# Bias rows of an attention kernel: twelve relu tiles moved to GpSimd, copies, relus and the first round dealt out anew

## The chip, the cores and the metric

The kernel runs on one core of a Trainium2 chip. The metric is device time in microseconds (us) for one launch; the median of three runs before the change is 658.66 us (657.89 to 660.17). PE is TensorE's matmul, PEld its weight load, DVE is VectorE, ACT is ScalarE, POOL is GpSimd, and SP issues most DMAs.

## The reference

The computation is attention with an additive bias that a small network makes from positions, followed by a feed-forward layer.

```python
scores = scale * np.matmul(q, k.transpose(0, 1, 3, 2))      # 4 batches, 8 heads, 576 x 576, head size 64
rel = (pos[:, None] - pos[None, :])
psi_rel = np.log1p(np.abs(rel))
psi_i = np.log1p(np.maximum(pos[:, None], 1.0))
x = (psi_rel / psi_i)[..., None]
h = np.maximum(x @ w1 + b1, 0.0)                            # 32 hidden units per pair of positions
bias = h @ w2                                               # 8 heads
scores = scores + bias.transpose(2, 0, 1)[None]
attn = softmax(scores);  out = attn @ v
# then, over 2304 tokens: h = x @ w_in (512 -> 2048), softplus(h), @ w_out (2048 -> 512)
```

## The kernel before

**Bias stage.** The bias is the same for all batches, so it is made once, for 576 query rows, in 36 sets of 16 rows. Dividing by `psi_i` is pulled out of the relu: for each group of four rows (a *quarter*, `g` 0 to 3, of set `s`) one relu tile `m` = max(lw + pb1, 0) is computed over the distances (`lw` has w1 times log1p of the distance, 128 partitions are 4 rows by 32 hidden units). That is 144 tiles of 304 to 576 columns. VectorE computes them (line 216), except those listed in `RELU_ACT`, which ScalarE computes (line 214). TensorE multiplies the four tiles of a set by the weights (line 243) into a PSUM tile `acc`, of which there are two. Then `emit_rows` copies `acc` to an SBUF tile `e`, times 1/psi_i: on ScalarE (line 267), or on VectorE (line 265) for the pieces in `EDVE`. A set in `MIR` (*mirrored*) is written by TensorE as a row of 591 columns in both directions, and one copy of 591 columns takes it; any other set is written once, and two copies take its two directions (591 columns together). A DMA (line 275) writes `e` to DRAM (`e_d`); the attention rounds read their bias tiles `b` from there, shifted row by row.

The order on every engine is the order of the program: nothing is rescheduled later. Set `s+1` is multiplied, set `s` copied, and the relus of set `s+5` are issued (`LEAD`) in each pass of the loop. `EARLY` says after which set a bias tile is loaded, and `STAGE` at which sets nine score tiles of the first round are put in between: D computes the softmax part (VectorE adds bias and takes the maximum, line 381; ScalarE exponentiates, line 399), R only copies the raw scores out (ScalarE, line 374).

**Rounds.** Sixteen rounds follow, one for each batch and pair of heads. A round is a string of tokens, written out by hand or by a search, that fixes the order on all engines: `Zt/b` and `St/b` are the score matmuls of tile t into PSUM buffer b (this round's and the next one's), `ZAt`/`At` VectorE's bias and maximum, `ZXt`/`Xt` ScalarE's exponential, `Tjc/b` six transposes on TensorE, `Vjc/a` or `/d` their copy to SBUF (tile `pt`) on ScalarE or VectorE (lines 332, 334), `Pj` the product with the values (line 486), `L`/`ZL` a small copy on GpSimd (line 416). Round 0 (`ROUND0`) has its own string, which also finishes the tiles that the bias stage began and begins those of round 1. Its tile 4 needs the bias rows of the last four sets. From round 1 on all rounds have the same string. The feed-forward layer follows on about 370 us of TensorE work.

Of the kernel before, what the change touches and what calls it, by code (L numbers as in the profile page):

```python
# [50 lines left out]
SETS = ((2, 4), (3, 8), (7, 5, 6), (1, 0))  # L51

ROUND0 = """
q Z7/0 S1/1 T10/o ZA7 A1 v1 Z3/0 T00/2 ZX7 ZA3 k S3/1 T20/0 V10/a X1 ZL2 T30/o A3 V30/d V00/a V20/a
Z8/0 A2 S8/1 ZX3 ZL1 X3 ZA8 T40/1 V40/a w S0/2 A8 A0 ZX8 X2 Z4/0 T32/0 ZA4 T12/o ZL3 T22/2 S4/1
V22/d X0 V12/d T02/1 ZX4 I V02/d V32/a v T01/2 L0 T11/o b V01/a V11/a T21/2 A5 R/0 A4 P0 A7 A6 V21/a
C X4 P1 ZL4 T31/2 X5 L4 X8 X6 T41/1 P2 L3 G L1 V31/d X7 L2 V41/d
"""

ROUND14 = """  # L60
# [41 lines left out]
NEAR = ("wi13", "wi14", "wi15", "wi3")  # L102
LEAD = 5

RELU_ACT = {(22, 2), (4, 3), (9, 2), (17, 3), (28, 3), (30, 3), (10, 3), (2, 2), (32, 3), (1, 3), (6, 2), (21, 3), (14, 3), (5, 3), (32, 2), (7, 3), (18, 3), (29, 3), (34, 2), (22, 3), (5, 2), (0, 3), (11, 3), (25, 2), (13, 3), (16, 2), (15, 3), (18, 2), (26, 3), (31, 2)}

LOAD_AT = {}
ORD = (0, 1, 2, 3, 4, 5, 6, 7, 8, 13, 9, 10, 11, 12, 14, 15, 16, 17, 18, 19, 20, 21, 22, 23, 24, 25, 26, 27, 28, 29, 30, 31, 32, 33, 34, 35)
MIR = (0, 1, 3, 4, 5, 6, 7, 8, 10, 13, 14, 15, 16, 18, 19, 21, 22, 24, 25, 29, 30, 33, 34, 35)
EDVE = {(34, 1), (24, 1), (27, 1), (33, 0), (35, 1), (7, 0), (29, 0), (19, 0), (14, 0), (8, 0), (3, 0), (27, 0)}  # L110
EARLY = ((24, 0), (12, 5), (21, 1), (17, 6), (27, 2), (26, 7), (33, 3), (35, 8))
STAGE = """
12:R12 21:R15 23:R16 23:R17 26:D06 28:D00 30:D01 32:D05 32:D02
"""


# [1 line left out]
def tile_log_bias_attention__then__softplus_ffn(  # L118
# [13 lines left out]
    nc = tc.nc  # L132
# [68 lines left out]
        return max(16 * s + 15, S - 1 - 16 * s) + 1  # L201

    hid, accs = {}, {}

    def emit_hid(j):
        if j >= 36:
            return
        s = ORD[j]
        w = width(s)
        for g in range(4):  # L210
            i = 4 * s + g
            m = mk.tile([128, S], F32, tag="m", name="m")
            if (s, g) in RELU_ACT:
                nc.scalar.activation(m[:, :w], lw[:, :w], AF.Relu, bias=pb1[:, i:i + 1])
            else:
                nc.vector.tensor_scalar(  # L216
                    m[:, :w], lw[:, :w], pb1[:, i:i + 1], 0.0, op0=ALU.add, op1=ALU.max
                )
            hid[s, g] = m

    def emit_mm(j):
# [33 lines left out]
    def emit_rows(j):  # L255
# [80 lines left out]
    def u_s(n, t):  # L336
# [41 lines left out]
        def first():  # L378
            m = st.tile([128, 1], F32, tag="m", name="m", bufs=12)
            st_["m"] = m  # L380
            nc.vector.tensor_tensor_reduce(  # L381
                prob[n, t].rearrange("p (a c) -> p a c", a=2),
                st_["ps"],
                bias[pr, t].rearrange("p (a c) -> p a c", a=2),
                op0=ALU.add,
                op1=ALU.min,
                scale=-0.125,
                scalar=3.0e38,
                accum_out=m,
            )  # L390
# [179 lines left out]
    def flush():  # L570
        run([((), None)] * 40)
# [497 lines left out]
```

## Time and profile before

| what | value |
|---|---|
| median of three runs | 658.66 us |
| profiled execution | 658.76 us, span 656.9 us |
| bias stage (first relu to last copy) | 5.4 to 55.6 us |
| round 0 up to its first product with the values | 55.6 to 66.9 us |
| PE busy over the span | 639.8 us, 97% |
| DVE, ACT, POOL busy over the span | 499.2, 509.1, 33.0 us |

Times in the trace count from the start of the span. A busy share over the whole span says little here: TensorE is full from 67 us on, and the change concerns what stands before. In a row that gives windows, each engine's busy time stands with the number of its instructions; in a row of waits stand the total, the times and the longest; a group of instructions shows busy time and the mean of one in ns, then the idle time before them.

### The profile page before, as it was taken

The page shows a single profiled execution, that of the slowest core. Times are in us where ns is not written, and L with a number is a line of the kernel's source. Part 1 is how long each engine was busy: PE and PEld are TensorE (multiplying, and loading weights), DVE is VectorE, ACT ScalarE, POOL GpSimd, SP SyncE. Part 2 cuts the span into 40 slices and gives each one's busy share as a digit, 9 for nine tenths or more (in the row PEclk, how much of TensorE's full clock was granted, in tenths as well). Part 3 has the DMA queues.
Part 4 walks back from the last instruction along what each step waited for, and adds up shares of the span by engine and source line. Part 5 has one row for each costly group of instructions (what it writes and reads, how often), then busy time and mean ns, then how long its engine had stood idle before and what let it go on. Part 6 is the DMA issues. An engine that isn't in the chain of part 4 may idle for free.

```text
span 656.9 us, 13575 instructions
## 1 busy us (share of the span) xinstructions
PE 639.8 (97%) x4992; PEld 483.2 (74%) x4992; DVE 499.2 (76%) x1081; ACT 509.1 (77%) x1034; POOL 33.0 (5%) x104
## 2 busy tenths in 40 slices
PE   6898999999999999999999999999999999999997
PEld 3334666766766766888888888888888888888886
DVE  7998799999999997896976847785964656556554
ACT  6998899999999997986877758866775665755653
POOL 0001111111111110000000000000000000000000
PEclk9999899999999999999999999999999999999999
DMA  6797889888886645752223004210201403202220
GB/s 223 274 312 251 287 257 315 266 257 277 274 257 231 192 155 177 234 204 95 100 96 121 8 30 165 96 65 32 81 16 56 132 7 113 80 1 88 73 97 32
DMA packets 51762, 98.97 MB, mean 151 GB/s; under 512 B 7520, under 2 KB 19440, under 8 KB 51696
## 3 DMA queue, kind: packets, MB, share of 16 engines
q1 hardware_dynamic: 51408, 98.03, 44.6%
q8 instruction: 39, 0.64, 0.4%
q14 instruction: 27, 0.22, 0.1%
q10 hardware_dynamic: 288, 0.07, 0.0%
HBM read 67.98 MB, written 28.01 MB: 146 GB/s over the span
## 4 chain that ended last, share of the span: by engine, by line
PE 95%; DMA 2%; DVE 1%; ACT 1%; issue 0%; SPq 0%; DVEq 0%; ACTq 0%
PE h L781 30%; PE y L839 30%; PE o L486 12%; PE s L363 6%; PE acc L243 5%; PE s L427 4%; PE t L363 3%; PE t L427 2%; DMA e_d<-e 1%; PE o L363 1%; PE o L427 1%; ACT e L267 1%; DMA wts<-in_mlp_dram 0%; DMA b<-e_d 0%; DVE p L381 0%
## 5 line engine op out<-in xcount | busy, mean ns | idle before, releaser
L839 PE MATMUL y<-wo,g 128*128 128x512 f32 x864 | 209.7, 390 | 0.0
L839 PEld LDWEIGHTS y<-wo,g 128*128 128x128 f32 x864 | 161.3, 188 | 33.4 <-DVE g L813 0.2
L781 PE MATMUL h<-x,wi 128*128 128x512 f32 (+1 forms) x768 | 169.6, 370 | 0.0
L781 PEld LDWEIGHTS h<-x,wi 128*128 128x128 f32 x768 | 136.2, 189 | 26.3 <-issue 0.5
L804 DVE SCALAR_TENSOR_TENSOR u<-u,e 128x512 f32<-128x512 f32 (+1 forms) x80 | 51.0, 638 | 102.5 <-ACT l L801 102.2
L399 ACT ACTIVATE p<-p,m 128x576 f32<-128x576 f32 x144 | 110.3, 767 | 4.4 <-DVE m L381 2.8
L797 ACT ACTIVATE e<-h 128x512 f32<-128x512 f32 (+1 forms) x80 | 44.3, 554 | 76.4 <-PE h L781 76.3
L486 PE MATMUL o<-pt,vn 128*64 128x256 f32 (+3 forms) x640 | 82.0, 421 | 0.0
L381 DVE CUSTOM_DVE_ANT_0 p<-s,b 128x576 f32<-128x576 f32 x83 | 61.3, 754 | 4.0 <-PE s L363 1.6
L811 ACT ACTIVATE g<-l 128x512 fp32r<-128x512 f32 (+1 forms) x80 | 46.8, 585 | 19.7 <-DVE l L808 9.8
L486 PEld LDWEIGHTS o<-pt,vn 128*64 128x64 f32 (+1 forms) x640 | 37.8, 137 | 28.0 <-issue 8.7
L363 PE MATMUL s<-kn,qn 64*128 64x288 f32 (+1 forms) x412 | 57.3, 413 | 0.7 <-ACT pt L332 0.4
L813 DVE TENSOR_TENSOR g<-l,g 128x512 fp32r<-128x512 f32 (+1 forms) x80 | 50.4, 629 | 3.7 <-ACT g L811 3.7
L808 DVE TENSOR_TENSOR l<-l,u 128x512 f32<-128x512 f32 (+1 forms) x80 | 50.6, 632 | 0.0
L806 DVE SCALAR_TENSOR_TENSOR l<-h,l 128x512 f32<-128x512 f32 (+1 forms) x80 | 50.5, 631 | 0.0
L332 ACT ACTIVATE pt<-s 128x384 f32<-128x384 f32 x93 | 44.3, 484 | 7.2 <-ACT r L537 4.9
L801 ACT ACTIVATE l<-u 128x512 f32<-128x512 f32 (+1 forms) x80 | 47.1, 589 | 2.9 <-DVE g L813 0.3
L800 ACT ACTIVATE u<-e 128x512 f32<-128x512 f32 (+1 forms) x80 | 47.2, 590 | 2.6
L798 ACT ACTIVATE e<-e 128x512 f32<-128x512 f32 (+1 forms) x80 | 47.2, 590 | 2.5
L243 PE MATMUL acc<-m,coef 128*32 128x512 f32 (+41 forms) x544 | 40.8, 429 | 8.5 <-DVE m L216 6.0
L427 PEld LDWEIGHTS s<-ident,p 64*128 64x128 f32 x654 | 31.1, 138 | 14.7 <-DVE m L381 8.4
L216 DVE TENSOR_SCALAR m<-lw,pb 128x576 f32<-128x576 f32 (+17 forms) x114 | 41.3, 440 | 0.0
(67 smaller groups left out, 750.9 us busy)
## 6 DMA issues: line engine op xcount, KB each, us to landing
e_d<-e SPq DMA_DIRECT2D x36, 295.5 KB, 3.5
qn<-in_q_dram SPq DMA_DIRECT2D x16, 576.0 KB, 6.6
b<-e_d SPq DMA_DIRECT2D x32, 288.0 KB, 3.9
r<-in_moe_w_in_dram SPq DMA_DIRECT2D x16, 512.0 KB, 5.0
r<-in_moe_w_out_dram SPq DMA_DIRECT2D x16, 512.0 KB, 3.8
xr<-x_d SPq DMA_DIRECT2D x28, 256.0 KB, 4.7
vn<-in_v_dram SPq DMA_DIRECT2D x16, 320.0 KB, 5.4
kn<-in_k_dram SPq DMA_DIRECT2D x16, 288.0 KB, 7.4
```

The lines of the kernel that those rows point to most:

```text
L243: nc.tensor.matmul(acc[32 * g:32 * g + 32, lo:hi], lhsT=coef.rearrange("p o h -> p (o h)"), rhs=m[:, d:d + hi - lo] if up > 0 else m[:, d ...
L363: nc.tensor.matmul(ps[at:at + w, half, :SH], lhsT=q_n[n][rows, hd, c0:c0 + w], rhs=k_n[n][rows, hd], start=True, stop=True, tile_position= ...
L381: nc.vector.tensor_tensor_reduce(prob[n, t].rearrange("p (a c) -> p a c", a=2), st_["ps"], bias[pr, t].rearrange("p (a c) -> p a c", a=2), ...
L399: nc.scalar.activation(p, p, AF.Exp, bias=st_["m"], scale=-1.0, accum_out=ssum[n][:, PLACE.index(t):PLACE.index(t) + 1],)
L427: nc.tensor.transpose(ps[:, a, i], src[rows], ident[rows, 64 * a:64 * a + 64], tile_position=(64 * a, 0))
L486: nc.tensor.matmul(o[up, half, 0:w], lhsT=v_n[n][rows, jb, hd], rhs=pt[n, jb][rows, c0:c0 + w], start=(jb == 0), stop=(jb == 4), tile_posi ...
L781: nc.tensor.matmul(ps[:, :nb], lhsT=wi[f][:, a, 128 * c:128 * c + 128], rhs=xs[bi, c][:, x_, :nb], start=(i == 0), stop=(i == 11),)
L804: nc.vector.scalar_tensor_tensor(u, u, -1.0, e, op0=ALU.add, op1=ALU.subtract)
L806: nc.vector.scalar_tensor_tensor(l, ps, 0.0, l, op0=ALU.max, op1=ALU.add)
L808: nc.vector.tensor_tensor(l, l, u, op=ALU.subtract)
L813: nc.vector.tensor_tensor(g[:, 1], l, g[:, 0], op=ALU.subtract)
L839: nc.tensor.matmul(y, lhsT=g[:, a, 128 * ts:128 * ts + 128], rhs=wo[f][:, w_], start=(first and i == 0), stop=(last and i == 2),)
```

## The change

Twelve relu tiles (`BESIDE`: loop pass, set, quarter) go to GpSimd. `beside()` issues those that are due, just ahead of a VectorE operation that reads PSUM (a copy in `EDVE` or a D tile's line 381) or else at the end of the pass; each is made to wait for the VectorE relu that was issued last before it (`held[-1]`). The other tables are dealt out anew: VectorE has 99 relus (114 before), ScalarE 33 (30), GpSimd 12 (0); `RELU_ACT` has a few entries that no longer apply, since `BESIDE` comes first. 26 sets are mirrored (24), so there are 46 copies (48): 37 on ScalarE (43) and 9 on VectorE (5). `EARLY`, `STAGE` and `ROUND0` are rearranged; the number of D tiles (five) and R tiles (four) in the stage is the same.

```diff
 ROUND0 = """
-q Z7/0 S1/1 T10/o ZA7 A1 v1 Z3/0 T00/2 ZX7 ZA3 k S3/1 T20/0 V10/a X1 ZL2 T30/o A3 V30/d V00/a V20/a
+Z7/0 S1/2 T10/o T00/1 ZA7 A1 A2 Z3/0 ZA3 ZX7 S3/1 Z8/0 k v1 ZL2 V10/a A3 T30/2 V30/d q X1 w V00/a
...
-RELU_ACT = {(22, 2), (4, 3), (9, 2), (17, 3), (28, 3), (30, 3), (10, 3), (2, 2), (32, 3), (1, 3), (6, 2), (21, 3), (14, 3), (5, 3), (32, 2), (7, 3), (18, 3), (29, 3), (34, 2), (22, 3), (5, 2), (0, 3), (11, 3), (25, 2), (13, 3), (16, 2), (15, 3), (18, 2), (26, 3), (31, 2)}
+RELU_ACT = {(4, 3), (28, 3), (0, 2), (8, 3), (33, 2), (13, 2), (32, 3), (1, 3), (15, 2), (26, 2), (21, 3), (4, 2), (12, 3), (17, 2), (19, 2), (10, 2), (32, 2), (1, 2), (16, 3), (29, 3), (12, 2), (20, 3), (23, 2), (14, 2), (5, 2), (27, 2), (29, 2), (9, 3), (31, 2), (33, 3), (13, 3), (24, 3), (35, 3), (7, 2), (26, 3), (20, 2)}
+BESIDE = ((17, 20, 2), (19, 21, 2), (23, 26, 2), (18, 22, 3), (20, 23, 0), (32, 35, 0), (21, 27, 0), (19, 22, 1), (24, 27, 3), (33, 35, 3), (27, 30, 0), (29, 33, 0))
+AFTER = mybir.DependencyInfo(mybir.DependencyClass.Sync, mybir.DependencyReason.ANTI)
-MIR = (0, 1, 3, 4, 5, 6, 7, 8, 10, 13, 14, 15, 16, 18, 19, 21, 22, 24, 25, 29, 30, 33, 34, 35)
+MIR = (0, 2, 3, 4, 5, 6, 7, 8, 10, 11, 12, 13, 14, 15, 16, 21, 22, 25, 26, 27, 29, 30, 32, 33, 34, 35)
-EDVE = {(34, 1), (24, 1), (27, 1), (33, 0), (35, 1), (7, 0), (29, 0), (19, 0), (14, 0), (8, 0), (3, 0), (27, 0)}
+EDVE = {(12, 1), (27, 1), (8, 0), (19, 0), (32, 0), (29, 1), (12, 0), (23, 0), (3, 0), (14, 0), (5, 0), (25, 0), (24, 1), (35, 1), (29, 0), (22, 0), (28, 1), (11, 0), (0, 0), (24, 0), (15, 0)}
-EARLY = ((24, 0), (12, 5), (21, 1), (17, 6), (27, 2), (26, 7), (33, 3), (35, 8))
+EARLY = ((23, 0), (10, 5), (18, 1), (19, 6), (29, 2), (26, 7), (33, 3), (35, 8))
-12:R12 21:R15 23:R16 23:R17 26:D06 28:D00 30:D01 32:D05 32:D02
+13:R15 20:D05 23:R12 24:R16 26:D06 27:R17 30:D01 31:D00 33:D02
...
+    def beside():
+        for s, g in queued.pop(now[0], ())[:]:
+            w = width(s)
+            i = 4 * s + g
+            m = mk.tile([128, S], F32, tag="m", name="m")
+            u = nc.gpsimd.tensor_scalar(
+                m[:, :w], lw[:, :w], pb1[:, i:i + 1], 0.0, op0=ALU.add, op1=ALU.max
+            )
+            tc.add_manual_dep(
+                u.ins, held[-1].ins.name, AFTER, reason="the port that both engines use"
+            )
+            hid[s, g] = m
...
+            if any(b[1:] == (s, g) for b in BESIDE):
+                continue
...
-                nc.vector.tensor_scalar(
+                held.append(nc.vector.tensor_scalar(
...
             if (s, part) in EDVE:
+                beside()
...
         def first():
             m = st.tile([128, 1], F32, tag="m", name="m", bufs=12)
             st_["m"] = m
+            beside()
...
+        now[0] = s
         emit_rows(s)
...
+        beside()
     flush()
```

GpSimd, from its last instruction of the set-up to the first small copies of round 0. `kn` is a one-column write that holds a load back, `m` a relu tile, `tl` a small copy of a probability tile `p`. Before:

```order
L294 COPY kn<-wts 128x1
L416 COPY tl<-p 128x128 x5
L416 COPY tl<-p_1031 128x128
L416 COPY tl<-p_1058 128x128
L416 COPY tl<-p 128x128 x3
```

Now:

```order
L316 COPY kn<-wts 128x1
L216 ISA
L216 TENSOR_SCALAR m<-lw,pb_112 128x336
L216 TENSOR_SCALAR m<-lw,pb_112 128x368
L216 TENSOR_SCALAR m<-lw,pb_112 128x352
L216 TENSOR_SCALAR m<-lw,pb_112 128x368
L216 TENSOR_SCALAR m<-lw,pb_112 128x384
L216 TENSOR_SCALAR m<-lw,pb_112 128x448
L216 TENSOR_SCALAR m<-lw,pb_112 128x432
L216 TENSOR_SCALAR m<-lw,pb_112 128x448
L216 TENSOR_SCALAR m<-lw,pb_112 128x496
L216 TENSOR_SCALAR m<-lw,pb_112 128x544
```

Two more relus of 576 columns follow, then the small copies as before; the row without a shape (ISA) stood ahead of line 673 before and now stands right behind the set-up.

VectorE in the middle of the stage, where the relus of sets 22 to 28 (368 to 464 columns) stand; `e<-acc` is a copy out of PSUM, `p,m<-s,b` a D tile. Before:

```order
L216 TENSOR_SCALAR m<-lw,pb_112 128x368 x2
L216 TENSOR_SCALAR m<-lw,pb_112 128x384 x4
L216 TENSOR_SCALAR m<-lw,pb_112 128x400 x4
L216 TENSOR_SCALAR m<-lw,pb_112 128x416 x3
L216 TENSOR_SCALAR m<-lw,pb_112 128x432 x3
L216 TENSOR_SCALAR m<-lw,pb_112 128x448 x4
L216 TENSOR_SCALAR m<-lw,pb_112 128x464 x3
L265 TENSOR_SCALAR e<-acc,tab 128x591
```

Now:

```order
L237 TENSOR_SCALAR m<-lw,pb_112 128x368 x2
L237 TENSOR_SCALAR m<-lw,pb_112 128x384 x2
L287 TENSOR_SCALAR e<-acc,tab 128x272
L237 TENSOR_SCALAR m<-lw,pb_112 128x400 x3
L237 TENSOR_SCALAR m<-lw,pb_112 128x416 x4
L237 TENSOR_SCALAR m<-lw,pb_112 128x432 x2
L404 ISA p,m<-s_83,b 128x576
L404 ISA m 128x1
L237 TENSOR_SCALAR m<-lw,pb_112 128x448
L287 TENSOR_SCALAR e<-acc,tab 128x208
L237 TENSOR_SCALAR m<-lw,pb_112 128x464 x3
```

Two copies and a D tile now stand between 17 relus, where 23 relus stood without a break.

ScalarE at the end of the stage. `e<-acc` are its last copies, `p,ss<-p,m` exponentials, `pt<-o` the first copy of transposes. Before:

```order
L267 ACTIVATE e<-acc,tab 128x591
L399 ACTIVATE p,ss_117<-p,m 128x576
L267 ACTIVATE e<-acc,tab 128x80
L267 ACTIVATE e<-acc,tab 128x511
L267 ACTIVATE e<-acc,tab 128x64
L267 ACTIVATE e<-acc,tab 128x527
L399 ACTIVATE p,ss_117<-p,m 128x576
L267 ACTIVATE e<-acc,tab 128x591
L399 ACTIVATE p,ss_117<-p,m 128x576 x4
L332 ACTIVATE pt<-o 128x2x3x64
```

Now:

```order
L289 ACTIVATE e<-acc,tab 128x591
L422 ACTIVATE p,ss_117<-p,m 128x576
L289 ACTIVATE e<-acc,tab 128x80
L289 ACTIVATE e<-acc,tab 128x511
L289 ACTIVATE e<-acc,tab 128x591 x3
L422 ACTIVATE p,ss_117<-p,m 128x576 x4
L354 ACTIVATE pt<-o 128x2x3x64
```

The copy of set 34, which VectorE made before, is now the third of the three and stands ahead of the four exponentials.

## Rows read from the trace of the kernel before

**Rows 1.** The page: the chain that ended last, shares by engine.

```profile
PE 95%; DMA 2%; DVE 1%; ACT 1%; issue 0%; SPq 0%; DVEq 0%; ACTq 0%
```

**Rows 2.** Windows: length; busy PE, PEld, DVE, ACT, POOL; clock, DMA share, GB/s.

```profile
5.40:55.60 50.20, 47.15 (x588) 19.13 (x588) 47.85 (x131) 46.15 (x87) 0.29 (x1) 1.00 0.81 287
...
46.20:55.60 9.40, 9.40 (x134) 4.02 (x132) 8.56 (x21) 8.10 (x18) 0.29 (x1) 1.00 0.80 289
55.60:66.90 11.30, 8.41 (x112) 5.18 (x110) 9.34 (x25) 9.28 (x24) 1.47 (x5) 0.98 0.79 268
```

**Rows 3.** Waits from 14 to 48 us: total, times, longest.

```profile
PEld acc L243 <- ACT e L267: 11.7, 21, 1.3
...
DVE e L265 <- PE acc L243: 1.5, 1, 1.5
ACT e L267 <- ACT e L267: 1.1, 2, 0.8
```

**Rows 4.** Groups of instructions in the stage, 5.4 to 55.6 us.

```profile
L216 DVE TENSOR_SCALAR m<-lw,pb 128x576 f32<-128x576 f32 (+17 forms) x114 | 41.3, 440 | 0.0
...
L267 ACT ACTIVATE e<-acc,tab 128x591 f32<-128x591 f32 (+22 forms) x43 | 25.5, 630 | 3.2 <-ACT e L267 1.4 <-PE acc L243 1.4 <-ACT m L214 0.2
L214 ACT ACTIVATE m<-lw,pb 128x496 f32<-128x496 f32 (+15 forms) x30 | 19.0, 661 | 3.4 <-DVE pb L192 3.4
...
L265 DVE TENSOR_SCALAR e<-acc,tab 128x591 f32<-128x591 f32 (+2 forms) x5 | 3.5, 707 | 2.0 <-PE acc L243 2.0
```

**Rows 5.** Groups by shape, 0 to 60 us: widest and narrowest copies.

```profile
L267 ACT ACTIVATE e<-acc,tab 128x591 f32<-128x591 f32 x21 | 15.7, 759 | 2.4 <-PE acc L243 1.4 <-ACT e L267 0.8 <-ACT m L214 0.2
...
L267 ACT ACTIVATE e<-acc,tab 128x47 f32<-128x47 f32 x1 | 0.3, 292 | 0.0
...
L265 DVE TENSOR_SCALAR e<-acc,tab 128x591 f32<-128x591 f32 x3 | 2.5, 832 | 2.0 <-PE acc L243 2.0
...
L265 DVE TENSOR_SCALAR e<-acc,tab 128x144 f32<-128x144 f32 x1 | 0.4, 363 | 0.0
```

**Rows 6.** Timeline of POOL: start, length; two operations of the relu's kind.

```profile
74.34 0.61 POOL L673 TENSOR_SCALAR a<-a 128x512 f32<-128x512 f32 x1 [1.90 <-ACT a L670]
...
87.03 0.61 POOL L673 TENSOR_SCALAR a<-a 128x512 f32<-128x512 f32 x1 [0.84 <-ACT a L670]
```

**Rows 7.** The chain of waits from 52 to 75 us: start, length.

```profile
55.58 3.81 DMA e_d<-e
...
59.53 2.74 DMA b<-e_d
...
63.64 0.76 DVE p L381
...
64.44 0.48 ACT p L399
...
66.92 3.54 PE o L486 x16
```

**Rows 8.** Timeline of ACT at the end of the stage.

```profile
52.44 0.78 ACT L399 ACTIVATE p<-p,m 128x576 f32<-128x576 f32 x1
...
53.19 0.77 ACT L399 ACTIVATE p<-p,m 128x576 f32<-128x576 f32 x1
...
56.26 0.78 ACT L399 ACTIVATE p<-p,m 128x576 f32<-128x576 f32 x1 [1.45 <-DVE m L381]
```

**Rows 9.** Timeline of DVE: its copy of set 34.

```profile
53.63 0.83 DVE L265 TENSOR_SCALAR e<-acc,tab 128x591 f32<-128x591 f32 x1 [0.24 <-PE acc L243]
```

**Rows 10.** Groups by shape, 0 to 130 us: copies of transposes on ACT.

```profile
L332 ACT ACTIVATE pt<-s 128x384 f32<-128x384 f32 x31 | 14.8, 485 | 2.4 <-ACT r L537 1.8 <-PE s L427 0.7
```

**Rows 11.** Timeline of PE: sixteen matmuls of one line, twice.

```profile
66.85 3.60 PE L486 MATMUL o<-pt,vn 128*64 128x256 f32 x16
...
74.29 1.89 PE L486 MATMUL o<-pt,vn 128*64 128x256 f32 x16
```

**Rows 12.** Windows around that stretch, columns as in rows 2.

```profile
66.40:69.80 3.40, 3.40 (x22) 1.93 (x24) 2.66 (x8) 2.55 (x8) 0.29 (x1) 0.50 1.00 382
```

More of the change, by code (lines that the diff above doesn't have):

```diff
@@ L53 @@
 ROUND0 = """
-q Z7/0 S1/1 T10/o ZA7 A1 v1 Z3/0 T00/2 ZX7 ZA3 k S3/1 T20/0 V10/a X1 ZL2 T30/o A3 V30/d V00/a V20/a
-Z8/0 A2 S8/1 ZX3 ZL1 X3 ZA8 T40/1 V40/a w S0/2 A8 A0 ZX8 X2 Z4/0 T32/0 ZA4 T12/o ZL3 T22/2 S4/1
-V22/d X0 V12/d T02/1 ZX4 I V02/d V32/a v T01/2 L0 T11/o b V01/a V11/a T21/2 A5 R/0 A4 P0 A7 A6 V21/a
-C X4 P1 ZL4 T31/2 X5 L4 X8 X6 T41/1 P2 L3 G L1 V31/d X7 L2 V41/d
+Z7/0 S1/2 T10/o T00/1 ZA7 A1 A2 Z3/0 ZA3 ZX7 S3/1 Z8/0 k v1 ZL2 V10/a A3 T30/2 V30/d q X1 w V00/a
+T20/0 S8/1 ZX3 ZL1 ZA8 X3 S0/o T40/2 X2 V20/a A8 ZX8 Z4/1 V40/a A0 T12/2 X0 V12/a T22/o ZA4 S4/1
+V22/d ZX4 ZL3 L0 T02/o v T32/0 V32/d T01/2 I b V02/a T11/o V01/a V11/a R/1 ZL4 C A5 A7 G T21/0 A4
+V21/a P0 A6 X8 P1 X5 X4 X6 T41/1 T31/0 L3 X7 L1 L2 P2 V41/d L4 V31/d
 """
@@ L203, in tile_log_bias_attention__then__softplus_ffn @@
     hid, accs = {}, {}
+    held, queued = [], {}
+    for at, s, g in BESIDE:
+        queued.setdefault(at, []).append((s, g))
+    now = [0]
+    def beside():
[10 more added lines that the diff above has]
+            hid[s, g] = m
     def emit_hid(j):
@@ L215, in emit_hid @@
             else:
-                nc.vector.tensor_scalar(
+                held.append(nc.vector.tensor_scalar(
                     m[:, :w], lw[:, :w], pb1[:, i:i + 1], 0.0, op0=ALU.add, op1=ALU.max
-                )
+                ))
             hid[s, g] = m
```

## The prediction

> **What bounds the kernel now.** I read the chain of waits first. TensorE has 95% of it [rows 1]; its last 590 us are full rounds and the feed-forward layer, and no line of the diff touches their order. What can move is the time at which round 0 hands TensorE its first product with the values, 66.9 us in this trace [rows 7]. Everything behind that shifts as a block. So I cut the time before it into windows [rows 2]: the bias stage (50.2 us) and round 0 up to that product (11.3 us).
>
> In the stage three engines look full: PE 47.15, DVE 47.85, ACT 46.15 of 50.2 us. PE's number deceives. The table of waits shows why: between 14 and 48 us its weight loads stand for 11.7 us, in 21 pieces, behind ScalarE's copy of line 267 [rows 3]. TensorE has two acc tiles, so set s+2 cannot begin until set s is copied, and that copy waits its turn between ScalarE's relus. VectorE and ScalarE are therefore the bound: at 47.85 / 50.2 = 95% and 46.15 / 50.2 = 92% they have 2.35 and 4.05 us to spare. In the last stretch, 46.2 to 55.6 us, TensorE never idles (9.40 of 9.40), while ACT has 1.3 us left.
>
> From the end of the stage to the product there is one chain [rows 7]: the last set's DMA to DRAM (55.58, 3.81 us), the load of bias tile 4 (59.53, 2.74 us), its maximum on VectorE (63.64), its exponential on ScalarE (64.44), transposes and copies, the product at 66.92. So a shorter stage is passed on whole, as long as the engines keep up with that chain.
>
> **The change part by part.**
>
> *VectorE.* It loses 15 relus: 41.3 us / 114 = 0.362 us each [rows 4], −5.4 us. It gains four copies; counted from the tables, its copies go from 2364 to 3898 columns. A copy costs (832 − 363) / (591 − 144) = 1.05 ns a column and 0.21 us besides [rows 5], of which some 0.09 us lies under its neighbour (an instruction's successor starts about that much before it ends). So 1534 columns and four starts are 1.6 + 0.5 = +2.1 us. Net −3.3 us.
>
> *ScalarE.* Three more relus: 661 ns less an overlap of 0.10 us, 0.56 us each [rows 4], +1.7 us. Six copies fewer with 1534 columns less: (759 − 292) / (591 − 47) = 0.86 ns a column and 0.25 us besides, 0.15 without the overlap [rows 5]: −1.3 − 0.9 = −2.2 us. Net −0.5 us.
>
> *The stage.* Together the two engines lose 3.8 of 94.0 us. At the same joint fill (94.0 of 100.4 us) the stage would be 90.2 / 94.0 of 50.2 us, which is 48.2: −2.0 us. The bounds come from the same rows. If ScalarE keeps its own fill of 92%, 45.65 / 0.919 gives 49.65 us, −0.55. If it is filled as VectorE was, 45.65 / 0.953 gives 47.9, −2.3. I take −2.0, nearer the second end, because VectorE, with 3.3 us less to do, can take the copies as they come, and because the unbroken run of 23 relus there is cut by two copies and a D tile, so that fewer sets wait for a ScalarE that is in the middle of its relus.
>
> *TensorE.* By the widths of the tables its columns in sets 27 to 35, where it never idles, go from 4907 to 5113. The last window (9.40 us) holds six sets and five score tiles, so a set of 591 takes under 1.57 us and 206 columns under 0.55 us; the other end is 0, where TensorE waits anyway. I take +0.1, since the score tiles have a large share of that window.
>
> *GpSimd.* Twelve tiles of 444 columns in the mean. Its operation of the same kind takes 0.61 us at 512 columns, both times the same [rows 6]: at most 7.3 us in a stage in which it now does nothing. By the table each is issued two to six passes before its set is multiplied, and a pass takes 50.2 / 36 = 1.4 us: being late by less than 2.8 us costs nothing. The waits stand in GpSimd's own queue, and nothing but the next relus is queued behind them until round 0's small copies. What a VectorE relu costs beside a GpSimd one no row shows: between nothing and a full stop for 7.3 us. I take 1 us, since by the tables seven of the twelve have an operation that reads PSUM next on VectorE; VectorE's 3.3 us cover it. Cost on the path: 0.
>
> The row without shape (ISA) that now stands behind the set-up stood before line 673. That operation's first run took 0.61 us like the second, and its wait of 1.90 us was for ScalarE's input [rows 6]; so I price it at nothing. The Trainium skill (GPSIMD Engine Reference, 2.1 Instruction dispatch) says that the first call after such a load pays about 6 us that no profile row shows. These rows leave no more than the 1.90 us for it; what the Trainium skill's figure would make of the time is the last rival.
>
> *Round 0.* It holds the same kinds of tokens in another order. Between its last copy of the stage and tile 4's exponential ScalarE has ten exponentials, as before, and five copies of transposes instead of four, but also set 34's copy. All of that fits into the time it idles there [rows 2], if the waits allow it. I take 0, with the third rival as the upper end and, as the lower, 0.8 us for the idle time that a better order could save.
>
> *Sum.* −2.0 + 0.1 = −1.9 us on the profiled 658.76 (span 656.9 and 1.9 around it): 656.9. The median of the three runs is 0.1 us under that execution, so **656.8 us**.
>
> **The rivals.**
>
> 1. *ScalarE stays the bound.* For it: TensorE's waits name ScalarE's copies, not VectorE's relus, and ScalarE is relieved by 0.5 us alone. Against: four copies leave its queue for VectorE at the very places where it bursts. Then −0.55 + 0.1: 658.2 us.
>
> 2. *The half-speed stretch goes.* From 66.4 to 69.8 us the granted clock is 0.50 [rows 12], the 1.2 GHz level, after a stretch in which PE was busy for 8.41 of 11.30 us. Sixteen products took 3.60 us there and 1.89 us a round later [rows 11]: 1.7 us lost, on the path. If the product starts 2 us earlier or round 0 is denser, TensorE may be busy enough not to be slowed. Against: the transposes before it are as thin as ever. Then 656.8 − 1.7 = 655.1 us.
>
> 3. *ScalarE late in round 0, slower than before.* Place: set 34's copy now stands on ScalarE ahead of four exponentials. VectorE began that copy at 53.63, when TensorE was done [rows 9], while ScalarE's exponentials began at 52.44 [rows 8]. From 53.63 on ScalarE has the copy (0.65), ten exponentials at 53.19 − 52.44 = 0.75 us [rows 8] and five copies of transposes (four at 485 − 100 ns, one narrower, 1.8 us [rows 10]): 63.6 us, only 0.8 before the 64.44 of the chain. It idled for 0.8 + 2.0 us there (from 54.81, the end of its wait of 1.45 us less that wait [rows 8], and in the round [rows 2]). If all of that idle time returns, the exponential comes at 66.4 and the product 2.0 us late; with rival 1's stage the result is 658.2 + 2.0 = 660.2. It decides as soon as the idle time kept is over 0.8 us. Against: that idle time was waiting for a chain that ScalarE was ahead of, so most of it should be swallowed.
>
> 4. *GpSimd stops VectorE.* If each of the twelve stops VectorE for its length, VectorE has −3.3 + 7.3 = +4.0 us, 1.65 more than its 2.35 us of idle time: 658.76 + 1.65 = 660.4. That five of the twelve have VectorE relus next, three of them released at one time, speaks for a part of it. The Trainium skill (SBUF — State Buffer, Who interferes with whom) gives the rule: VectorE's fast SBUF mode and GpSimd share one pair of ports, and the second to start waits for the whole of the first; an operation with one SBUF input outside that mode is free of it. By it only the unsheltered tiles count, some five times 0.5 us, and the sum on the path stays 0. No row of this trace has the two side by side.
>
> 5. *The first GpSimd tile is late.* Set 20's tile is issued in pass 17, so its start-up may cost 4.2 us (three passes) before TensorE stands still; every us beyond is one on the path. For the rows' 1.90 us that is nothing. By the 6 us of the Trainium skill (GPSIMD Engine Reference, 2.1 Instruction dispatch), as an estimate, it is 6 − 4.2 = 1.8 us, and the time 658.6 us.
>
> **How the numbers follow.** The forecast has 0.46, rival 1 0.14, rival 2 0.21, rival 3 0.11, rivals 4 and 5 0.04 each. About 0.3% (2.0 us) is what a measurement of this kernel can tell from no change, so faster means below 656.7 and slower above 660.6. The forecast sits on the first line: 0.22 of it falls under and 0.24 over. Faster: 0.22 + 0.20 of rival 2 + 0.01 = 0.43. Slower: half of rivals 3 and 4 (0.07) and 0.03 for a second half-speed stretch (+1.7 us): 0.10. The rest, 0.47, is no change. The range leaves out the far ends: from rival 2 less 0.4 to rival 3 less 0.4, **654.7 to 659.8**.
>
> **What would show it.** Right: the last copy ends near 53.6 us, the waits of weight loads for ScalarE's copies between 14 and 48 us fall well under 11.7, GpSimd's tiles take 0.45 to 0.7 us and end before TensorE wants them, the product starts near 65. Wrong: ScalarE fuller than 95% with the last copy still past 55 (rival 1); no window at clock 0.5 (rival 2); idle PE before the product with ScalarE as releaser (rival 3); VectorE relus far longer than 0.5 us beside GpSimd (rival 4). A first product that starts where it did would make the whole prediction wrong.

## The result

The kernel after the change takes 663.85 us (median of 6 runs, 662.10 to 665.38) against 658.45 us (6 runs) for the kernel before: a ratio of 1.0077, 95% interval 1.0063 to 1.0092. It is slower by 5.4 us. The forecast was 656.8 us, 654.7 to 659.8, with a chance of 0.10 for slower: wrong in sign, and the time lies outside the range.

In the profile after (span 662.0 us), first the chain that ended last, as in [rows 1]:

```profile
PE 90%; DMA 4%; ACT 2%; DVE 1%; issue 1%; POOL 1%; SPq 0%; DVEq 0%; ACTq 0%
```

TensorE's share of the chain fell from 95% to 90%, and GpSimd is on it. Next the windows of the stage, which now lasts to 60.4 us, and of the stretch with the low clock, with the columns of [rows 2] and [rows 12]:

```profile
5.40:60.40 55.00, 48.88 (x604) 19.27 (x604) 48.25 (x121) 45.92 (x84) 23.23 (x13) 1.00 0.76 264
...
66.00:70.00 4.00, 3.70 (x36) 2.01 (x36) 2.95 (x9) 4.00 (x13) 0.74 (x3) 0.62 0.80 232
```

The last copy ends at 60.35 us, not 55.55. The first product with the values, on which the prediction hung the whole time, starts 5.6 us later than in [rows 11]:

```profile
72.49 2.16 PE L509 MATMUL o<-pt,vn 128*64 128x256 f32 x16
```

The span is 5.1 us longer, so what stands behind that product did shift nearly as a block. In the stage TensorE was idle for 6.1 us (55.00 − 48.88) where it had been for 3.05. The fifth number points to the cause: POOL is busy for 23.23 us, against 0.29. The groups of GpSimd's relus (30 to 60 us) and of VectorE's (30 to 56 us) in after:

```profile
L216 POOL TENSOR_SCALAR m<-lw,pb 128x368 f32<-128x368 f32 (+8 forms) x12 | 22.9, 1924 | 30.4 <-ACT e L289 25.7 <-PE acc L264 3.1 <-DVE m L237 1.6
...
L237 DVE TENSOR_SCALAR m<-lw,pb 128x416 f32<-128x416 f32 (+13 forms) x34 | 16.7, 553 | 0.0
```

And VectorE's group of before from 30 to 56 us:

```profile
L216 DVE TENSOR_SCALAR m<-lw,pb 128x384 f32<-128x384 f32 (+13 forms) x44 | 17.0, 460 | 0.0
```

A GpSimd tile takes 1.92 us in the mean; the prediction had 0.61 at most. The last two rows say more: VectorE has ten relus fewer in that stretch and saves 0.3 us, because each became longer (553 ns against 460). The waits from 30 to 60 us (total, times, longest) name the new releaser, which [rows 3] did not have:

```profile
PEld acc L264 <- POOL m L216: 3.9, 4, 1.5
...
PE acc L264 <- POOL m L216: 2.4, 4, 1.0
```

The chain of after, where [rows 7] had one DMA of 3.81 us and one of 2.74, has longer ones; the load at 58.06 of a bias tile waits for the rows issued at 53.14:

```profile
42.73 2.37 POOL m L216
...
53.14 4.84 DMA e_d<-e
...
58.06 5.14 DMA b<-e_d
```

Up to set 20 TensorE begins the sets within about 1 us of the trace of before; from then on the relu that ends last in sets 20 to 23, 26, 27, 30, 33 and 35 is GpSimd's. Its last one ended at 58.18 us, TensorE's last product of the stage a microsecond later. The chain above leaves the stage earlier, with the rows issued at 53.14 us: it passes tiles of the eight that stand back to back and none of the last four.

### The profile page after: what moved, and what is told of

Its sections match the earlier page's. It is cut to its first block, busy times and chain, and to the rows that moved or that the text cites. A ratio compares the mean times of both kernels' runs of the same rounds, so it can differ in the third digit from the quotient of the medians.

```text
span 662.0 us, 13590 instructions
## 1 busy us (share of the span) xinstructions
PE 641.4 (97%) x5008; PEld 483.6 (73%) x5008; DVE 498.7 (75%) x1069; ACT 508.6 (77%) x1032; POOL 56.0 (8%) x116
## 4 chain that ended last, share of the span: by engine, by line
PE 90%; DMA 4%; ACT 2%; DVE 1%; issue 1%; POOL 1%; SPq 0%; DVEq 0%; ACTq 0%
PE h L804 30%; PE y L862 30%; PE o L509 11%; PE s L385 6%; PE s L450 4%; PE t L385 3%; PE acc L264 3%; PE t L450 1%; DMA b<-e_d 1%; PE o L385 1%; ACT e L289 1%; DMA e_d<-e 1%; PE o L450 1%; DMA r_d<-r 1%; POOL m L216 1%
## 5 line engine op out<-in xcount | busy, mean ns | idle before, releaser
L509 PE MATMUL o<-pt,vn 128*64 128x256 f32 (+3 forms) x640 | 80.6, 416 | 0.0
L264 PE MATMUL acc<-m,coef 128*32 128x512 f32 (+44 forms) x560 | 42.3, 420 | 11.5 <-DVE m L237 6.1
L264 PEld LDWEIGHTS acc<-m,coef 128*32 128x32 f32 x560 | 15.9, 114 | 35.8 <-issue 11.7
L385 PEld LDWEIGHTS s<-kn,qn 64*128 64x128 f32 (+1 forms) x408 | 31.4, 172 | 13.9 <-issue 4.6
```

Of the source, the lines that this page charges most:

```text
L264: nc.tensor.matmul(acc[32 * g:32 * g + 32, lo:hi], lhsT=coef.rearrange("p o h -> p (o h)"), rhs=m[:, d:d + hi - lo] if up > 0 else m[:, d ...
L385: nc.tensor.matmul(ps[at:at + w, half, :SH], lhsT=q_n[n][rows, hd, c0:c0 + w], rhs=k_n[n][rows, hd], start=True, stop=True, tile_position= ...
L509: nc.tensor.matmul(o[up, half, 0:w], lhsT=v_n[n][rows, jb, hd], rhs=pt[n, jb][rows, c0:c0 + w], start=(jb == 0), stop=(jb == 4), tile_posi ...
```

## The experiments

Theory A said that the form of GpSimd's operation is slow by itself, B that GpSimd and VectorE disturb each other, C that the new deal loses without GpSimd. The table gives each kernel's median, that of the kernel before on the same chip, and the ratio with its interval; e4, run once to time single forms, has no ratio.

| kernel | us | before | ratio |
|---|---|---|---|
| e1 twelve tiles on VectorE | 663.30 | 658.76 | 1.0060 (1.0047 to 1.0073) |
| e2 twelve tiles on GpSimd, all else old | 661.66 | 658.76 | 1.0046 (1.0031 to 1.0062) |
| e3 constant instead of the column | 663.46 | 658.76 | 1.0066 (1.0054 to 1.0078) |
| e5 new round 0 alone | 658.98 | 658.76 | 0.9997 (0.9985 to 1.0009) |
| e6 new stage alone, tiles on VectorE | 661.77 | 658.76 | 1.0038 (1.0024 to 1.0051) |
| e7 maximum with a column | 665.18 | 658.76 | 1.0087 (1.0068 to 1.0106) |
| e8 after with the old round 0 | 662.22 | 658.76 | 1.0057 (1.0038 to 1.0076) |
| e9 after with clamps | 661.65 | 658.37 | 1.0049 (1.0036 to 1.0062) |
| e10 tiles issued early | 665.74 | 658.37 | 1.0107 (1.0091 to 1.0122) |
| e11 before with clamps | 657.98 | 658.37 | 1.0004 (0.9990 to 1.0019) |
| e12 e9, old score tiles and round 0 | 659.49 | 658.96 | 1.0011 (0.9993 to 1.0028) |
| e13 e11 with new score tiles | 662.46 | 658.96 | 1.0044 (1.0027 to 1.0061) |
| e14 e9 with the old round 0 | 660.67 | 658.96 | 1.0022 (1.0013 to 1.0032) |
| e15 e9, 32 tiny matmuls first | 661.79 | 658.87 | 1.0049 (1.0036 to 1.0063) |
| e16 e6, 32 tiny matmuls first | 661.81 | 658.87 | 1.0044 (1.0031 to 1.0057) |
| e17 before, 100 tiny matmuls first | 664.10 | 658.87 | 1.0082 (1.0067 to 1.0096) |

**e1, e2: the change halved.**

```diff
+RELU_ACT -= {b[1:] for b in BESIDE}     # e1
+BESIDE = ()
```

e2 is the kernel after with `RELU_ACT`, `MIR`, `EDVE`, `EARLY`, `STAGE` and `ROUND0` of before.

> The kernel after, with its twelve GpSimd relus given to VectorE instead; copies, relus on ScalarE, mirrored sets and round 0 stay as dealt anew. VectorE then has 111 relus against 114 before (-1.1 us) and four more copies (+2.1), ScalarE -0.5 us: +0.5 us on 94.0 us of work, so the stage is at most 0.3 us longer than before. Theory A (the loss is what GpSimd's tiles take) and theory B (the loss is that GpSimd and VectorE disturb each other): both expect 659 us, 657.5 to 660.5. Theory C (the loss lies in the new deal and order, GpSimd only shows it): it stays at 662 us or more.

> The kernel before with its own deal and its own round 0, and only the twelve tiles moved to GpSimd at the same passes as in the kernel after. Theories A and B: the tiles are late here too, since eight of them stand back to back on GpSimd from pass 17 on, so the last copy of the stage ends 3 to 5 us later and the time is 661 to 664 us. Theory C: VectorE is relieved of about eleven relus (4 us) and the time is at most 658.5 us.

Each half loses by itself: GpSimd's tiles in the old deal 2.9 us, the new deal without them 4.5. So A or B holds for one half and C for the other. In e1 VectorE is busy for 14.02 of 14.20 us from 32 to 46.2 us: with 111 relus on VectorE this does not test the deal by itself, for which e9 was made.

**e3, e4, e7: what makes GpSimd's tile slow.**

```diff
-                m[:, :w], lw[:, :w], pb1[:, i:i + 1], 0.0, op0=ALU.add, op1=ALU.max
+                m[:, :w], lw[:, :w], 0.25, 0.0, op0=ALU.add, op1=ALU.max                        # e3
+                m[:, :w], lw[:, :w], npb[:, i:i + 1], F64_INF, op0=ALU.max, op1=ALU.min         # e7
```

In e7 `npb`, the negative of the column, is made once ahead of the stage.

> The kernel after with one thing changed: GpSimd adds the constant 0.25 in its twelve tiles, where it added a column of one scalar per partition (so these tiles leave out their true bias). Theory A (the form with the column of scalars is slow by itself, about 3.8 ns an element of a row): the twelve tiles take 0.4 to 0.7 us each as line 673 of before does, TensorE no longer waits for them, and the time is the forecast's 656.8 us (655 to 659). Theory B (any GpSimd tile beside VectorE's relus is slow): they stay at 1.5 to 2.2 us and the time at 662 us or more.

> The kernel before with GpSimd operations added whose results nobody reads: at 1 to 4 us, when VectorE does nothing, one relu with a column of scalars and one with a constant (352 columns); from 5 us on, beside VectorE's unbroken relus, the same two, the maximum alone with either scalar, the clamp of line 673, an addition of two inputs, and a copy, at 352, 176 and 352 columns. Theory A: with the column of scalars 1.5 us at 352 columns also alone, with a constant 0.45 us both times. Theory B: alone both take 0.45 us, beside VectorE all forms 1.3 us or more. A mixture (slow by itself and slower beside VectorE) shows in the difference between the two stretches. The time of the whole says nothing here.

> The kernel after with GpSimd's twelve tiles in another form: the larger of the distances and the negative column, then the smaller of that and a large constant. Each differs from the relu by one constant for each row, which the softmax takes out. In the run with forms side by side an addition followed by a maximum took 1.47 us at 352 columns alone, with a column or a constant alike, and a minimum followed by a maximum 0.49 to 0.54. Theory A' (the pair of operations sets the price): 0.5 to 0.8 us a tile, no wait of TensorE for GpSimd, the last copy near 54 us. Rival (the column of scalars has a price of its own beside it): 1.2 us or more a tile. The time follows from round 0 as well: with theory R 660.5 us, with theory S 657.

e3 missed: with a constant the tiles stay slow (1.94 us at 448 columns, 2.13 at 576). e7 missed too (2.20 us at 576). The groups of e4 say what counts; L222 ran at 1.3 to 4.2 us, before VectorE's relus, the rest beside them, `z<-z,zc` has the column and `z<-z` a constant; L214 and L222 are an addition and a maximum, L216 a maximum alone, L217 a minimum and a maximum, both with constants, L218 an addition of two inputs, L219 a copy:

```profile
L214 POOL TENSOR_SCALAR z<-z,zc 128x352 f32<-128x352 f32 x2 | 3.3, 1656 | 0.1
L214 POOL TENSOR_SCALAR z<-z 128x352 f32<-128x352 f32 x2 | 3.1, 1528 | 0.2
L216 POOL TENSOR_SCALAR z<-z,zc 128x352 f32<-128x352 f32 x2 | 2.6, 1310 | 0.2
L216 POOL TENSOR_SCALAR z<-z 128x352 f32<-128x352 f32 x2 | 2.3, 1130 | 0.2
L218 POOL TENSOR_TENSOR z<-z,zc 128x352 f32<-128x352 f32 x2 | 1.6, 802 | 0.2
L222 POOL TENSOR_SCALAR z<-z,zc 128x352 f32<-128x352 f32 x1 | 1.5, 1468 | 0.1
L222 POOL TENSOR_SCALAR z<-z 128x352 f32<-128x352 f32 x1 | 1.4, 1385 | 0.1
L219 POOL COPY z<-z 128x352 f32<-128x352 f32 x2 | 1.1, 535 | 0.1
L217 POOL TENSOR_SCALAR z<-z 128x352 f32<-128x352 f32 x2 | 1.0, 516 | 0.2
```

The relu's form takes 1.47 us with nothing beside it and 1.66 in the mean beside VectorE (1.80 and 1.51): theory A, slow by itself, and B adds an eighth. But A named the wrong reason: the column costs the relu 0.08 us. The clamp between two constants, 516 ns, is the exception, and it was the operation of [rows 6]. That the pair of functions alone sets the price, as A' had it, e7 rules out: a maximum and a minimum, with the column, are as slow as the relu. Why the clamp is fast is not shown.

e4 also shows what GpSimd costs VectorE: its relus from 5.4 to 27 us in e4,

```profile
L235 DVE TENSOR_SCALAR m<-lw,pb 128x528 f32<-128x528 f32 (+12 forms) x39 | 21.4, 624 | 0.0
```

and in before:

```profile
L216 DVE TENSOR_SCALAR m<-lw,pb 128x320 f32<-128x320 f32 (+17 forms) x62 | 21.9, 432 | 0.0
```

Beside 21 GpSimd operations (21.4 us from first to last) VectorE got through 39 relus in the time of 62, of which the later ones are narrower. Once GpSimd was done, VectorE's relus stayed 6.9 us later than in before, 0.4 of which stood before the first of them: 6.5 us, or 0.31 us for each operation in the mean over all these forms, nearly the 0.36 us that moving a relu away was to save.

**e10: the same tiles, earlier.**

```diff
+BESIDE = tuple(sorted((s - 6, s, g) for _, s, g in BESIDE))
```

> The kernel after with GpSimd's twelve tiles, of the form and the length as they are, issued in the sixth pass before the one that copies their set (before: two to four passes), so that they are spread from pass 14 to 29. GpSimd's 23 us then fit beside 50 us of stage. Theory L (what costs is that the tiles come late, not that they are long): TensorE waits for GpSimd for less than 1 us in all, the last copy comes at 55 to 57 us, the time is 658.5 to 660.5. Rival B (what counts is that VectorE's relus take up to 0.75 us beside them): the last copy past 58 us and 662 us or more.

It does not tell lateness from length: the first tile began at 28.63 us, only 2 us before the 30.58 of after, and the twelve took 24.7 us, nine of them without a gap. What held the first one back is not shown (it waits for TensorE, VectorE and ScalarE, for ScalarE last; a relu buffer that must come free would do that). The last copy came at 59.66 us. The numbers are rival B's. GpSimd, not the pass of issue, sets the pace, and the waits of TensorE's weight loads for it rose to 5.3 us from 28 to 60 us.

**e5, e6, e8: round 0 and the stage.** `ROUND0` alone is swapped: in before (e5), in e1 (e6), in after (e8).

> The kernel before with the new order of round 0 alone (the stage, its copies and relus as before, nothing on GpSimd). In the kernel after without GpSimd's tiles the stage's last copy came 1.8 us later than before and the end of the program 5.2 us, so 3.4 us arose behind the stage. Theory R (the new order of round 0 is slower by itself): 661 to 662.5 us. Theory S (the stage's new end, with its late last sets, makes round 0 late; the order does no harm): 658.8 us, 657.8 to 659.8, and the prediction's price of 0 stands.

> The kernel after with the twelve tiles on VectorE and with the old order of round 0: of the change only the new copies, relus of ScalarE, mirrored sets, early loads and score tiles of the stage are left. Theory R: the stage's last copy 1.8 us later and no more, 660.5 us (659.8 to 661.2). Theory S: as with the new order, 663 us.

> The kernel after with the old order of round 0 and all else as it is, GpSimd's tiles included. Theory R: the 4.8 us by which the last copy is late stay, less what the order cost (3 us): 661 us. Theory S: 663.5 us, the same as after.

The new order costs nothing in the old kernel (e5: theory S, the prediction's 0), but some 1.3 to 1.5 us behind the new stage: after against e8, e1 against e6. e6 and e8 came out a little above what theory R expected and below what S did; neither is right as put. The cost of round 0 depends on the stage in front of it; what part the clock has in it follows with e14.

**e9, e11: GpSimd's tile made cheap.**

```diff
-                m[:, :w], lw[:, :w], pb1[:, i:i + 1], 0.0, op0=ALU.add, op1=ALU.max
+                m[:, :w], lw[:, :w], F64_INF, 0.0, op0=ALU.min, op1=ALU.max
```

> The kernel after with GpSimd's twelve tiles as a clamp between two constants, the very pair of operations of line 673 (these tiles leave out their bias). In the run with forms side by side that pair took 0.49 to 0.54 us at 352 columns. Theory P (the prediction failed on the price of GpSimd's tile alone; its other terms hold): tiles of 0.45 to 0.7 us, the last copy near 53.6, the time 657 us (655.5 to 658.5). Theory Q (the new deal of copies and relus loses by itself, as the 661.8 us without GpSimd's tiles suggest; there VectorE was busy for 14.00 of 14.20 us from 32 to 46.2): tiles as fast, the last copy still past 55.5, and 659 to 661.5 us. Rival B (VectorE beside GpSimd is what counts): 662 us or more.

> The kernel before with its own deal and round 0 and the twelve tiles on GpSimd as the same clamp (these tiles leave out their bias). About ten relus less on VectorE (3.7 us), nothing late. If VectorE bounds the stage of before, as the prediction held (95% of it), the last copy comes 1 to 2 us earlier and the time is 657 us (656 to 658). If the chain of two acc tiles and ScalarE's copies bounds it, 658.7 us as before.

These run the prediction's own assumption. Groups of GpSimd's tiles and of VectorE's relus (30 to 56 us) in e9:

```profile
L216 POOL TENSOR_SCALAR m<-lw 128x576 f32<-128x576 f32 x2 | 1.3, 666 | 2.8 <-DVE m L237 2.8
L216 POOL TENSOR_SCALAR m<-lw 128x448 f32<-128x448 f32 x2 | 1.1, 560 | 1.2 <-DVE m L237 1.2
...
L237 DVE TENSOR_SCALAR m<-lw,pb 128x416 f32<-128x416 f32 (+12 forms) x32 | 12.9, 466 | 0.0
```

And e9's windows, of the stage and of its last stretch:

```profile
5.40:56.20 50.80, 46.91 (x604) 18.28 (x605) 45.11 (x121) 45.51 (x83) 7.24 (x12) 1.00 0.82 282
...
46.20:55.60 9.40, 9.39 (x141) 3.86 (x138) 6.30 (x16) 6.84 (x15) 1.94 (x3) 1.00 0.73 261
```

The twelve tiles take 0.47 to 0.92 us, 7.2 in all, and VectorE's relus are hardly stretched (466 ns in the mean). VectorE has 2.7 us less work than in [rows 2], and the stage still ends at 56.13 us, 0.6 later than before, theory Q, though the time of 661.65 is a little over its range. The last row shows one half of why: TensorE is full (9.39 of 9.40 us, as it was before) while VectorE is busy for 6.30. The other half are TensorE's own waits from 5.4 to 55.6 us, in before and in e9:

```profile
PE acc L243 <- DVE m L216: 6.0, 1, 6.0
PE acc L243 <- ACT e L267: 2.2, 5, 0.9
```

```profile
PE acc L264 <- DVE m L237: 6.1, 1, 6.1
PE acc L264 <- ACT e L289: 3.0, 7, 0.7
```

The wait for VectorE is the one ahead of the first product, most of it before the window. Behind it TensorE waited for ScalarE's copies alone, and with the new deal not less but more. e11 says the same of the old deal: eleven relus less on VectorE brought the last copy from 55.55 to 54.78 (0.4 of that stood at set 4 already, long before the first clamp) and the time nothing that can be measured: its median of 657.98 us lies in the range expected if VectorE bounds, but before took 658.37 beside it, and the ratio is 1.0004.

**e12, e13, e14: which part of the deal.** `STAGE`, `EARLY` and `ROUND0` of before in e9 (e12), of after in e11 (`STAGE` and `EARLY` only, e13), `ROUND0` of before in e9 (e14).

> The kernel after with GpSimd's twelve tiles as a clamp of constants (they leave out their bias), the old round 0, and the score tiles and early bias loads of the stage where they stood before; copies, relus and mirrored sets are the new ones. With clamps and the new score tiles, sets 25 to 29 took 6.6 us on TensorE against 4.5 before, and three score tiles (R16, D06, R17) stood there instead of one. Theory K (the place of the score tiles cost that): the last copy at 54.3 to 55.3 us, 657 to 658.5 us in all. Rival M (the mirrored sets and the copies dealt anew cost it): the last copy at 55.8 us or later, 659 us or more.

> The kernel before with the same clamps on GpSimd (they leave out their bias), its own round 0, copies, relus and mirrored sets, but the score tiles and early loads of the stage where the kernel after has them. Without that last edit the last copy came at 54.8 us and the time was 658.0. Theory K: the last copy at 55.5 to 56.5 us, 659 to 660 us. Rival M: 54.5 to 55.2 us, 658 us.

> The kernel after with the same clamps (they leave out their bias) and the old round 0. With the new round 0 it took 661.65 us, last copy at 56.1, with two stretches of 3.4 us at half the clock in the profiled run. If the new round 0 costs time only behind a late stage, by a later landing of the last bias rows and by more half-speed stretches: 659.5 to 660.5 us with the last copy still at 56.1. If it costs nothing: 661.5 us.

Neither K nor M stands alone. Last copies: 54.78 (e11), 56.50 (new copies and sets, e12), 55.95 (new score tiles, e13), 56.79 (both, e14). These are single traces: e9 and e14 have the same stage and differ by 0.7 us, which stand from set 6 on, so smaller differences say little. In the times the two parts do not add up: 1.0004, 1.0011, 1.0044, and 1.0022 with both. Where the time goes between sets 25 and 29, TensorE's groups show, in before (39.99 to 44.52 us) and in e9 (38.77 to 45.40):

```profile
L243 PE MATMUL acc<-m,coef 128*32 128x176 f32 (+4 forms) x40 | 3.9, 496 | 0.2 <-ACT e L267 0.2
L363 PE MATMUL s<-kn,qn 64*128 64x288 f32 x6 | 1.2, 437 | 0.0
```

```profile
L264 PE MATMUL acc<-m,coef 128*32 128x176 f32 (+6 forms) x56 | 4.6, 439 | 0.2 <-ACT e L289 0.2
L385 PE MATMUL s<-kn,qn 64*128 64x288 f32 x14 | 2.7, 447 | 0.0
```

The stretch is 2.1 us longer because TensorE has that much more to do in it, three score tiles instead of one and more mirrored sets; it waits for 0.2 us in both. By set 30, ahead of which before has its next score tile, 1.3 us of it are left. e9 had reached set 25 1.2 us earlier. So the new tables put work of TensorE where it is full, and leave it more idle time where it had some.

e14 against e9 came out near what was expected of an order that costs time only behind this stage: 1.0022 against 1.0049, some 1.8 us, with 660.67 us just over the range. Their granted clocks differ: e9's trace has 6.8 us at the 1.2 GHz level, e14's 3.4. The window around that stretch in e9,

```profile
64.00:71.00 7.00, 6.17 (x60) 3.96 (x62) 4.50 (x13) 4.81 (x12) 0.70 (x3) 0.51 1.00 348
```

and in e14:

```profile
69.00:72.60 3.60, 3.60 (x16) 1.57 (x16) 2.12 (x8) 2.97 (x9) 0.29 (x1) 0.53 1.00 372
```

The mean granted clock of e9's runs is 0.991 to 0.995, of nearly all of e14's 0.997. So it is wherever the new round 0 costs time: the mean over the runs is 0.9932 in e9 and 0.9968 in e14, 0.9926 in e1 and 0.9971 in e6, 0.9973 in after and 0.9988 in e8, while e5, where it costs nothing, has 0.9981 and before 0.9976. Times the span of 660 us these differences are, as an estimate, up to 2.4, 3.0 and 1.0 us, against steps of 1.8, 1.5 and 1.3. Of after's own runs the three at 0.999 or more took 662.10 to 663.48 us, the other three 664.21 to 665.38. So the lower clock can account for most of what the new round 0 costs; that it is the whole cause is not shown, since e15 below takes e9's time with 0.9968. The other link that was expected, a later landing of the last rows, is not seen: 61.08 us in e9, 62.06 in e14.

Why the clock fell longer is not shown either: in e5, whose TensorE was as thinly used, it did not fall from 56 to 76 us. Two windows of e5, clock 1.00:

```profile
60.00:64.00 4.00, 1.94 (x30) 0.98 (x26) 2.48 (x7) 4.00 (x11) 0.79 (x3) 1.00 0.64 183
64.00:68.00 4.00, 3.08 (x48) 2.03 (x50) 3.04 (x11) 2.61 (x8) 0.38 (x2) 1.00 1.00 356
```

**e15, e16, e17: a load of instructions in the way of the last rows.** The DMA of set 35's rows landed 3.0 to 5.9 us after its issue (taken to the start of the load that waits for it, some 0.1 us behind). In nine traces it followed by some 1.75 us the end of a 16 KB packet of the instruction queue, as in e9: packet 58.32 to 59.30, landing 61.08.

```diff
+        for _ in range(32 if j == 0 else 0):
+            nc.tensor.matmul(
+                acc[0:32, 0:16], lhsT=one, rhs=one[:, 0:16],
+                start=True, stop=True, tile_position=(0, 0),
+            )
         for lo, hi, d, up in parts:
```

> The kernel after with GpSimd's twelve tiles as clamps (they leave out their bias) and the new round 0, as in the run of 661.65 us, plus 32 tiny matmuls (64 TensorE instructions) in the idle time before set 0. In nine traces the DMA of the last bias rows landed 1.7 to 1.9 us after the end of a 16 KB load of instructions on one DMA engine wherever that load ended 2.6 us or more after the DMA's issue, in six others it landed after 3.0 to 4.6 us. One such load comes for every 256 of TensorE's instructions. Theory F (the load holds back one part of that DMA): 64 instructions more move the load from 58.3 us to about 55, ahead of the last rows; they land after 3 to 4 us instead of 4.9, and the time falls by about 1 to 1.9 us, to 660.2. Rival (the landing depends on the traffic of the early bias tiles, the load only stands beside it): landing 4.9 us, 661.6.

> The same 32 tiny matmuls in the kernel that has of the change only the new stage, with the twelve tiles on VectorE and the old round 0 (661.77 us, last rows landing after 4.9 us, load of instructions at 59.4). Theory F: the load at about 56, landing after 3 to 4 us, 660.3 us. Rival: landing 4.9 us, 661.8.

> The kernel before with 100 tiny matmuls in the idle time before set 0 (200 instructions), which brings the load that stood at 71 us to about 57.5 us, into the landing of the last rows (from 55.6). Theory F: landing at about 60.5 instead of 59.5, the time 1 us longer, 659.7. Rival: no change of the landing, 658.8 us.

The landing moved as theory F said: 4.0 us in e15 (4.9 in e9), 4.1 in e16 (4.9 in e6). Its price did not: the times stayed. In e15 the next packet (62.13 to 63.10) stood in the load of tile 4, and the chain has the gain given back there:

```profile
56.20 3.88 DMA e_d<-e
...
60.78 3.88 DMA b<-e_d
```

In e9 itself the chain does not pass the last rows, but the load of another bias tile, issued 0.4 us behind them:

```profile
56.52 5.05 DMA b<-e_d
```

So this load of instructions goes with a late landing, in the two cases as forecast, and does not decide the time. e17 says nothing on it: the hundred matmuls delayed set 0 to 11.54 us, the stage ended at 60.20, and the packet fell ahead of the rows.

## Why the prediction was wrong, point by point

**GpSimd, cost on the path 0: the step that failed first.** "Its operation of the same kind takes 0.61 us" took the row of another operation for the price. [rows 6] is a minimum and a maximum with constants; the relu is an addition and a maximum, and GpSimd takes about three times as long for it (e4), also before VectorE begins. In after the old row is unchanged:

```profile
78.69 0.62 POOL L696 TENSOR_SCALAR a<-a 128x512 f32<-128x512 f32 x1 [0.44 <-ACT a L693]
```

Twelve tiles are 22.9 us and not 7.3; the eight between passes 17 and 24 alone take 14.5 us back to back, so an allowance of 2.8 us each does not help. That allowance was a pass too long besides: a set is multiplied in the pass before the one that copies it, so the tiles have one to five passes and not two to six, and set 20's tile has two and not three (rival 5). The price of the true tiles against clamps, all else equal, is 1.8 us in after and e9 (1.0077 against 1.0049), 2.3 in e8 and e14, 2.8 in e2 and e11. The first is the least, and e9 has the lowest clock of these; after's last copy comes 4.2 us after e9's, but its chain leaves the stage ahead of that. The bounds on this price should have been wide: no row of before had this operation on GpSimd.

**GpSimd beside VectorE: taken 1 us, measured 3.0.** At e9's pace (12.9 / 32) the 34 relus would have taken 13.7 us of VectorE; they took 16.7. That lies within the bounds of 0 to 7.3, but it eats most of VectorE's relief. Rival 4, at 0.04, had the direction; the full stop that it described is not seen. The Trainium skill (SBUF — State Buffer, Who interferes with whom) has VectorE, in its two-port mode, wait for the whole of GpSimd's instruction when that started first. Here four of VectorE's relus ended while GpSimd's tile of 42.73 to 45.09 us ran, and the relus of 464 columns took 670 ns against 455, so the trace does not agree with a full stop.

**The stage, −2.0 us by the same joint fill: the step that failed second, and without GpSimd's doing.** "PE's number deceives" was the error. [rows 2] has TensorE idle for 3.05 of 50.2 us, 0.6 of that before its first product: to end 2.0 us earlier nearly all the rest had to go, and in the last 9.4 us there was none. VectorE was relieved nearly as forecast (e9: 45.11 us against 47.85, −2.7 of −3.3), and the fill of both engines simply fell. −2.0 was the price of an engine for which TensorE did not wait behind its first product; e9's trace measured +0.6, e14's with the same stage +1.2. Rival 1 named the engine that TensorE waits for, ScalarE, whose copies held it for 3.0 us instead of 2.2, though ScalarE is no fuller than it was (45.51 of 50.80 us). The waits of weight loads for these copies, on which the prediction built, fell from 11.7 only to 10.3 us in after (14 to 48 us); the matmuls themselves stood still for them for 2.2 us in the whole stage of before.

**TensorE +0.1.** Too small as far as it was seen: with the new copies and mirrored sets the last copy came 1.7 us later (e12 against e11), some 0.8 of which stood at set 19 already, and the last window of TensorE is as full in e9 as it was in before. The sum counted the columns of sets 27 to 35 and not the score tiles, of which six instead of five now stand behind set 25. How much of it is the added columns was not measured alone; the prediction's upper end was 0.55.

**Round 0: 0.** Right for the order alone (e5), wrong behind the new stage (1.3 to 1.8 us), where it comes with a lower clock that can account for most of it. In after's chain behind the stage stand the DMAs of bias rows, not rival 3's exponentials. Rival 2 came with the opposite sign in e9, as a longer stretch at the 1.2 GHz level. After's own trace has one of 3.4 us, as before.

**The start-up of GpSimd, 0: right.** In after the first tile took 1.73 us at 336 columns, the third 1.56 at 352. The Trainium skill (GPSIMD Engine Reference, 2.1 Instruction dispatch) speaks of about 6 us for the first call of a freshly loaded kernel; no run here shows it: in e4 the first operation started at 1.30 us, 0.1 us after the configuration, and took 1.47 us.

The ladder of ratios, each kernel against before beside it, sums up where the 5.1 to 5.4 us are: cheap tiles in the old deal 1.0004 (e11), the new copies and sets 1.0011 (e12), the new score tiles 1.0022 (e14), the new round 0 1.0049 (e9), the true tiles 1.0077. Only the last two steps are larger than their intervals, and e13 shows that the order of the steps matters: the new score tiles cost 2.6 us in the old deal. What stays open is why the granted clock fell longer with the new round 0 behind the new stage, and whether anything but the clock makes the step from e14 to e9. No version tried beats the kernel before by more than the noise.

## What to carry to other kernels

Price an operation from a row of the same operation, with the same pair of functions and the same kind of scalars: on GpSimd two tensor-scalar operations of equal shape differed threefold. Before crediting relief of an engine, subtract the bottleneck's busy time from the stretch and ask for whom it waits in the rest: here 2.2 us of waits for ScalarE's copies were all there was to win, and relief of VectorE did not touch them. A helper engine that slows the one it helps has to be charged for it: here a GpSimd operation cost VectorE some 0.3 us (e4) to save 0.36. When two versions differ by a microsecond or two, compare their granted clocks before looking for the link that made it.

## What the runs showed of the hardware that was not expected

- GpSimd at 128 x 352, means of e4's groups: addition and maximum 1.39 to 1.66 us, a maximum alone 1.13 to 1.31, two inputs added 0.80, a copy 0.54, a clamp between two constants 0.52.
- VectorE's relus of 464 columns took 670 ns in the mean beside GpSimd's relus and 455 beside its clamps.
- One 16 KB packet of the instruction queue held one DMA engine for 0.9 to 2.8 us; in nine traces the last rows landed about 1.75 us after its end. There were 39 such packets for TensorE's 10,016 instructions in after, one for 257.
